# mLSTM attention and two feed-forward stages on one core: the values' product in three 16-bit products, small VectorE work on GpSimd in the source's order, last weight rows loaded once, a fifth row buffer

## The chip, the cores and the metric

The kernel runs on one core of a Trainium2 chip (trn2). The metric is the device time of one execution in microseconds; a kernel's time is the median of its runs. In a profile the engines are PE (TensorE, with PEld for its weight loads), DVE (VectorE), ACT (ScalarE), POOL (GpSimd) and SP (SyncE, which here only issues DMAs). Each engine works through its own queue in order.

## What is computed

Three stages follow each other. First a gated recurrent attention over B, H, S, D = 4, 8, 768, 40; then a feed-forward layer over all 3072 tokens (320 to 2048 to 320 with x·sigmoid(x)); then a mixture of 8 experts (320 to 1024 to 320), in which each token goes to one expert.

```python
for t in range(S):                                  # attention, all b and h
    m_new = np.maximum(f_gate[:, :, t] + m, i_gate[:, :, t])
    f_stab, i_stab = np.exp(f_gate[:, :, t] + m - m_new), np.exp(i_gate[:, :, t] - m_new)
    C = f_stab[:, :, None, None] * C + i_stab[:, :, None, None] * np.einsum('bhd,bhe->bhde', vt, kt)
    n = f_stab[:, :, None] * n + i_stab[:, :, None] * kt
    y[:, :, t] = o * (C @ qt) / np.maximum(np.abs(n @ qt), 1.0)
x = y.transpose(0, 2, 1, 3).reshape(B * S, H * D)
h = x @ w_in;  x = (h / (1 + np.exp(-h))) @ w_out   # first feed-forward layer
expert = argmax(x @ w_gate)                         # the mixture
out = gate * (np.maximum(x @ w1[expert], 0) @ w2[expert])
```

## The kernel before, in words

**Attention** is done in chunks of 128 steps: 6 chunks `c` times 4 batches `b`, so 24 units, each with all 8 heads. A unit has these parts. `prep_qk` splits k and q into 16-bit high and low halves and turns them with a DMA transpose. `load_lam` and `mask_lam` fetch and mask a 128x1024 table of log weights (the mask on POOL, L207), `prep_exp` takes its exponent on ACT (eight instructions, L241). `at_S` multiplies k by q on PE (two groups of four heads), and DVE multiplies the product by the weights in place (L296), which gives the float32 matrix P in the `lam` buffer. `at_I` adds what earlier chunks left (L304, L308). `at_C` updates the state C (24 16-bit products of 41 columns, L353 to L355; before it DVE multiplies the old state by a decay, L359; afterwards L367, L370, L375 and two DMAs). **`at_PV` multiplies P by v in float32** (L318, eight products, two PE passes each), then DVE divides (L324 to L340) and copies 64 columns (L341). `at_X` turns the result for the next stage (L394).

**The first layer** runs over 6 chunks of 512 tokens and 16 blocks `f` of 128 hidden columns. For each block, `l1` does eight 512-column products (L959), ACT the tanh (L975), DVE the product (L978), ACT the 16-bit high half (L983), DVE the low half (L986), and `l2`, two blocks later, twelve products of 328 columns (L1003 to L1005; in part of chunk 0 float32, L1000).

**What sets the order.** The attention of chunk c+1 runs beside the first layer of chunk c. The table `plan` gives each part a position; `f` has two positions, so one chunk has 32. A unit starts (`at_S`) at its position p, eight after the one before it; what a part returns runs one position later (`run_late`). Chunk 0 is ordered by a scheduler; from chunk 1 on PE, ACT, DVE and SP run in the source's order (`by_hand`, L1060), while POOL's order is still the scheduler's. The routing of a finished chunk, `rows`, is put at positions 5, 7, ... 19 of the next chunk, two apart: `experts`, `scale`, `weights`, `place` (two PE products, L877 and L878, into one of the two `ps_at` buffers), then four `halves`, each of which makes a row of 386 words on ACT and DVE (L919 to L928) and scatters it with an indirect DMA from POOL (L929) into `rows_x`.

**The experts** come last: 28 slots of 128 rows. For a slot, `fetch` reads a register, turns 128 rows with a DMA transpose (L1189) and gets two columns (L1194), `m_half` does 32 products of 128 columns (L1209) twice, `m_l2` 24 of 320 columns (L1228 to L1230), and POOL scatters the result (L1240). Rows have four buffers (`xT_b`, L1182): `get(i + 3)` fetches for three slots ahead. Beside this, weights of the experts that don't fit are loaded in 32 pieces by `load_w` (three DMAs: two thirds of w1, **its last 64 rows twice, into both halves of the partitions**, and w2), split on ACT (L552, L553) and DVE (L556 to L564). All these DMAs are on SP's queue:

```python
for i in range(2, len(line)):
    get(i + 3)
    t = half(i, 0); low_and_load(); t()
    if i > 5 and i % 2: split()
    t = half(i, 1); t()
    if i > 5 and i % 2: low_and_load()
    if i == 3: later_slots()
    split()
    if more and i > 4: load(more.pop(0))
    second(i - 1)
```

Of the kernel before, what the change touches and what calls it, by code (L numbers as in the profile page):

```python
# [19 lines left out]
SQ = 256.0  # L20
SX = 2.0**8
# [12 lines left out]
def mlstm_moe_kernel(ctx, tc, q, k, v, ig, fg, og, w_in, w_out, w_gate, w1, w2, out):  # L34
# [106 lines left out]
    q_ld, k_ld, o_ld = [turns([carve(ATTN, (H, D)) for _ in range(3)]) for _ in range(3)]  # L141
# [10 lines left out]
    y_b = turns([carve(FIRST, (384,)), const.tile([128, 384], F32, name="y2")])  # L152
# [133 lines left out]
    def at_S(c, b, g):  # L286
        u = st[c, b]
        if c == 0:
            ps = ps_l1.tile([128, 4, CH], F32, tag="l1", name="ps_s")
        else:  # L290
            ps = ps_at.tile([128, 4, CH], F32, tag="at", name="ps_s")
        for j in range(4):
            h = 4 * g + j
            nc.tensor.matmul(ps[:, j, :], u["kT"][0:120, h, :], u["qT"][0:120, h, :], start=True, stop=True)
        lt = u["lam"][:, 4 * g:4 * g + 4, :]
        return lambda: nc.vector.scalar_tensor_tensor(  # L296
            out=lt, in0=ps, scalar=1.0 / (SQ * SQ), in1=lt, op0=ALU.mult, op1=ALU.mult
        ) and None
# [15 lines left out]
    def at_PV(c, b):  # L314
        u = st[c, b]
        pv = ps_at.tile([128, H, D1], F32, tag="at", name="ps_pv")
        for h in range(H):
            nc.tensor.matmul(pv[:, h, :], u["lam"][:, h, :], u["v"][:, h, :], start=True, stop=True)  # L318

        def tail():  # L320
# [12 lines left out]
            nc.vector.tensor_scalar(out=den, in0=den, scalar1=1.0, scalar2=2.0, op0=ALU.max, op1=ALU.mult)  # L333
# [7 lines left out]
            nc.vector.tensor_copy(out=yt[:, DM:384], in_=yt[:, 256:DM])  # L341
# [3 lines left out]
    def at_C(c, b):  # L345
# [11 lines left out]
        if c > 0:  # L357
            o = c * BH + b * H
            nc.vector.tensor_tensor(  # L359
# [172 lines left out]
    def load_w(k, g, e, ts=None):  # L532
# [6 lines left out]
        if isinstance(e, int):  # L539
            nc.sync.dma_start(out=t[:, 0:2, :], in_=w1[e, 0:256, cs].rearrange("(j p) f -> p j f", p=128))  # L540
            nc.sync.dma_start(out=t[:, 2, :], in_=bcast0(w1[e, 256:320, cs], 2))
            nc.sync.dma_start(out=t2, in_=w2[e, cs, :].rearrange("(j p) d -> p j d", p=128))
        else:
            ee = bass.ds(e, 1)
            nc.sync.dma_start(out=t[:, 0:2, :], in_=w1[ee, 0:256, cs].rearrange("e (j p) f -> p (e j) f", p=128))
            nc.sync.dma_start(out=t[:, 2, :], in_=w1[ee, 256:320, cs].to_broadcast([2, 64, GF]))
# [4 lines left out]
        def go():  # L551
            nc.scalar.activation(out=o1[:, 0:3, :], in_=t, func=AF.Copy, scale=SW1)  # L552
            nc.scalar.activation(out=o2[:, :, 0, :], in_=t2, func=AF.Copy, scale=SW2)  # L553

            def tail():
# [5 lines left out]
                    out=o1[64:128, 2, :], in0=t[64:128, 2, :], scalar=SW1, in1=o1[64:128, 2, :],  # L561
# [9 lines left out]
    with contextlib.nullcontext():  # L571

        wg_t = const.tile([128, 3, E], F32, name="wg_t")
        with tc.tile_pool(name="gate", bufs=1) as gp:
# [105 lines left out]
            def first(b, g):  # L680
                return first_d(b, g, sel, parts, idb, mneg)

            run = lambda ts: [t() for t in ts]
# [24 lines left out]
            v0 = prep_v(0, 0)  # L708
            p0 = at_PV(0, 0)
# [8 lines left out]
            v1 = prep_v(0, 1)  # L718
            p1_ = at_PV(0, 1)
# [20 lines left out]
            v2 = prep_v(0, 2)  # L740
            p2 = at_PV(0, 2)
# [13 lines left out]
            v3 = prep_v(0, 3)  # L755
            p3 = at_PV(0, 3)
# [19 lines left out]
                out=E_t[:, 1:, :], in0=E_t[:, 1:, :], scalar1=1.0 / (SQ * SQ), scalar2=None, op0=ALU.mult  # L776
# [20 lines left out]
        for n in range(B, NC * B):  # L797
# [8 lines left out]
            at(p - 5, mask_lam, *cb)  # L806
            at(p - 3, prep_exp, *cb, 0)
            at(p - 2, prep_exp, *cb, 1)
            at(p, at_S, *cb, 0)
            at(p + 1, at_S, *cb, 1)  # L810
# [33 lines left out]
        def rows(c, b0=0, b1=B):  # L844
# [70 lines left out]
            def halves(b):  # L915
# [5 lines left out]
                def tail():  # L921
# [21 lines left out]
        at(2 * NF * (NC - 1) + 23, lambda: fetch_early())  # L943
# [238 lines left out]
        xT_b = turns([x[:, 0:6, :] for x in Ks[1:] + Qs + Ks[:1]])  # L1182
# [115 lines left out]
        with tc.manual_schedule(engines=by_hand):  # L1298
# [29 lines left out]
            get(NE + 1)  # L1328
            for i in range(2, len(line)):
                get(i + 3)  # L1330
# [57 lines left out]
```

## Time and profile before

| | us |
|---|---|
| median of 3 runs (lowest to highest) | 732.72 (732.57 to 733.4) |
| the profiled execution, its own time | 736.41 |
| its span on the core | 734.7 |
| PE busy in the span | 671.2 (91%) |
| DVE busy | 529.7 (72%) |
| ACT busy | 372.7 (51%) |
| POOL busy | 100.6 (14%) |
| PE, first layer's L959 | 193.1 |
| PE, values' product L318 | 51.2 (modelled, 384 pieces) |
| PE, experts' L1209 | 110.0 (1792 pieces) |

Busy time is the union of an engine's instructions. PE's instructions overlap in their pipeline, so a piece that reads 0.3 us can follow the one before it 0.14 us later: what a product costs is read from the distance between starts, not from its length. The span is cut into stages by the instructions that run in it: attention alone up to about 47 us, first layer with attention up to about 435, first layer alone up to about 509, experts up to 723, and then the last scatter.

### The profile page before, as it was taken

To read this page: it belongs to the slowest core of one execution; us is meant where nothing else is said; L and a number is where in the kernel's file an instruction comes from. 1 tells how busy PE (TensorE), PEld (TensorE's weight loads), DVE (VectorE), ACT (ScalarE), POOL (GpSimd) and SP (SyncE) were. 2 spreads that over 40 slices of the span, in tenths; PEclk is the share of its full clock that TensorE was granted. 3 is DMA by queue.
4 is the path that set the end of the run, shared out by engine and by line. 5 is a ranking of instruction groups with operands and counts; after the bars stand their busy time and mean duration, and the time that the engine had idled before them with its cause. 6 is when DMAs were issued, how large, how long until landed. Compare 5 with 4: busy or idle time off the path is not lost.

```text
span 734.7 us, 15579 instructions
## 1 busy us (share of the span) xinstructions
PE 671.2 (91%) x5840; PEld 480.0 (65%) x5840; DVE 529.7 (72%) x1262; ACT 372.7 (51%) x816; POOL 100.6 (14%) x134
## 2 busy tenths in 40 slices
PE   3868899999899989998999999999999898998993
PEld 2734666776476655665666665556888786877882
DVE  7775779987888787799887975975677655665631
ACT  4644365655575655675676635564334333533410
POOL 3100011100121002110210110020311111111111
PEclk9758599999999988999999999999999999999998
DMA  8768979884565655976587520544279799999900
GB/s 158 128 150 205 201 144 212 196 198 88 106 139 127 138 100 106 166 149 131 116 180 162 133 80 14 128 146 105 80 145 194 166 189 171 186 170 190 160 24 15
DMA packets 242828, 102.82 MB, mean 140 GB/s; under 512 B 181141, under 2 KB 236632, under 8 KB 242744
## 3 DMA queue, kind: packets, MB, share of 16 engines
q1 hardware_dynamic: 239380, 92.98, 63.8%
q0 software_dynamic: 2880, 8.68, 3.5%
q8 instruction: 48, 0.79, 0.5%
q14 instruction: 36, 0.29, 0.2%
q10 hardware_dynamic: 484, 0.08, 0.1%
HBM read 71.64 MB, written 11.59 MB: 113 GB/s over the span
## 4 chain that ended last, share of the span: by engine, by line
PE 70%; DVE 13%; DMA 8%; ACT 3%; SPq 3%; issue 2%; POOL 0%; POOLq 0%; DVEq 0%; ACTq 0%
PE ps_h L959 19%; PE ps_m L1209 12%; PE ps_y L1003 5%; PE ps_y L1005 5%; PE ps_y L1004 5%; PE ps_pv L318 5%; DMA Ks<-rows_x 3%; PE ps_y L1000 3%; PE ps_m L1228 3%; PE ps_m L1230 3%; PE ps_m L1229 3%; DMA Qs<-rows_x 2%; PE ps_wg L517 1%; DMA wi<-in_moe_w_in_dram 1%; DMA w_all<-lam_d 1%
## 5 line engine op out<-in xcount | busy, mean ns | idle before, releaser
L959 PE MATMUL ps_h<-w_all 128*128 128x512 f16 x768 | 193.1, 392 | 8.2 <-ACT w_all L466 5.1
L959 PEld LDWEIGHTS <-w_all 128*128 128x128 f16 x768 | 73.5, 100 | 85.1 <-issue 10.6
L1209 PEld LDWEIGHTS <-w_all 128*128 128x128 f16 x1792 | 106.8, 101 | 19.1 <-DMA Ks<-rows_x 9.9
L1005 PE MATMUL ps_y<-w_all 128*128 128x328 f16 x332 | 101.1, 305 | 0.3 <-DVE w_all L986 0.3
L1004 PE MATMUL ps_y<-w_all 128*128 128x328 f16 x332 | 101.1, 305 | 0.0
L1003 PE MATMUL ps_y<-w_all 128*128 128x328 f16 x332 | 100.9, 305 | 0.0
L1214 ACT ACTIVATE hh<-ps_m 128x512 f16<-128x512 f32 x56 | 33.3, 596 | 126.5 <-PE ps_m L1209 114.9
L975 ACT ACTIVATE w_all<-ps_h 128x512 f32<-128x512 f32 x83 | 49.2, 592 | 67.0 <-PE ps_h L959 66.8
L978 DVE SCALAR_TENSOR_TENSOR w_all<-w_all,ps_h 128x512 f32<-128x512 f32 x83 | 56.7, 683 | 29.3 <-ACT w_all L975 28.0
L1215 DVE SCALAR_TENSOR_TENSOR hl<-ps_m,hh 128x512 f16<-128x512 f32 x56 | 38.6, 690 | 48.5 <-ACT hh L1214 48.1
L983 ACT ACTIVATE w_all<-w_all 128x512 f16<-128x512 f32 x83 | 51.6, 622 | 30.7 <-DVE w_all L978 28.9
L1229 PE MATMUL ps_m<-w_all,hh 128*128 128x320 f16 x224 | 67.0, 299 | 0.0
L1230 PE MATMUL ps_m<-w_all,hl 128*128 128x320 f16 x224 | 67.0, 299 | 0.0
L1228 PE MATMUL ps_m<-w_all,hh 128*128 128x320 f16 x224 | 67.0, 299 | 0.0
L1209 PE MATMUL ps_m<-Ks,w_all 128*128 128x128 f16 x896 | 55.9, 226 | 8.9 <-DMA Ks<-rows_x 6.9
L986 DVE SCALAR_TENSOR_TENSOR w_all<-w_all 128x512 f16<-128x512 f32 x83 | 57.9, 697 | 5.6 <-ACT w_all L983 5.3
L1209 PE MATMUL ps_m<-Qs,w_all 128*128 128x128 f16 x896 | 54.1, 222 | 6.0 <-DMA Qs<-rows_x 4.2
L1240 POOL DMA_INDIRECT out_dram<-ym,sid x28 | 32.0, 1142 | 169.5 <-DVE sid L1239 153.7
L318 PEld LDWEIGHTS ps_pv<-w_all 128*128 128x128 f32 x384 | 51.2, 210 | 4.3 <-issue 1.7
L318 PE MATMUL ps_pv<-w_all 128*128 128x41 f32 x384 | 51.2, 296 | 0.4 <-DVE w_all L296 0.4
L241 ACT ACTIVATE w_all<-w_all,bias_t 128x128 f32<-128x128 f32 x160 | 50.2, 391 | 2.4 <-POOL w_all L207 2.3
L207 POOL TENSOR_SCALAR_AFFINE_SELECT w_all<-w_all 128x1024 f32<-128x1024 f32 x20 | 22.8, 1142 | 183.1 <-DMA w_all<-lam_d 130.0
(219 smaller groups left out, 1159.6 us busy)
## 6 DMA issues: line engine op xcount, KB each, us to landing
e<-in_moe_w_dram SPq DMA_DIRECT2D x35, 320.0 KB
w_all<-lam_d SPq DMA_DIRECT2D x20, 512.0 KB
e<-in_moe_w_dram SPq DMA_DIRECT2D x35, 256.0 KB
w_all<-in_moe_w_out_dram SPq DMA_DIRECT2D x16, 320.0 KB
e<-in_moe_w_dram SPq DMA_DIRECT2D x35, 128.0 KB
w_all<-in_moe_w_dram SPq DMA_DIRECT2D x13, 320.0 KB
wi<-in_moe_w_in_dram SPq DMA_DIRECT2D x8, 512.0 KB
w_all<-in_k_dram SPq DMA_DIRECT2D x24, 160.0 KB
```

Source lines behind the costliest of these rows:

```text
L318: nc.tensor.matmul(pv[:, h, :], u["lam"][:, h, :], u["v"][:, h, :], start=True, stop=True)
L959: nc.tensor.matmul(ps, a, x, start=(i == 0), stop=(i == len(terms) - 1))
L978: nc.vector.scalar_tensor_tensor(out=th, in0=th, scalar=1.0, in1=ps, op0=ALU.add, op1=ALU.mult)
L983: nc.scalar.activation(out=gh, in_=th, func=AF.Copy, scale=SG)
L986: nc.vector.scalar_tensor_tensor(out=gl, in0=th, scalar=SG, in1=gh, op0=ALU.mult, op1=ALU.subtract)
L1003: nc.tensor.matmul(ps, gh[:, ts], woh[:, f, :], start=(f == 0), stop=False)
L1004: nc.tensor.matmul(ps, gh[:, ts], wol[:, f, :], start=False, stop=False)
L1005: nc.tensor.matmul(ps, gl[:, ts], woh[:, f, :], start=False, stop=(f == NF - 1))
L1209: nc.tensor.matmul(ps[:, jj, :], w1c[k][:, a, f * 128:f * 128 + 128], x[:, m, :], start=(n == 0), stop=(n == len(terms) - 1),)
L1228: nc.tensor.matmul(ps, hh[:, f, :], w[:, 0, :], start=(f == 0), stop=False)
L1229: nc.tensor.matmul(ps, hh[:, f, :], w[:, 1, :], start=False, stop=False)
L1230: nc.tensor.matmul(ps, hl[:, f, :], w[:, 0, :], start=False, stop=(f == NF2 - 1))
```

## The change

1. **Values' product.** P is scaled by 64 and split on its way: ACT copies it to 16 bit (`ph_b`, one buffer for all units), POOL subtracts that from P and leaves the 16-bit rest in the `lam` buffer. v is split likewise by `split_v`, at position p (ACT high half, DVE low half). `at_PV` then has three 16-bit products for each head in place of one float32 product. The scale is taken out with the denominator.
2. **POOL** takes the decay of C (L359), the copy of 64 columns of y (L341) and the three copies of a row (L926 to L928). From chunk 1 on its order is the source's as well. The mask moves from position p-5 to p-4; `rows` come at 5, 7, 9, 13, 14, 16, 18, 20.
3. **Weights.** The last 64 rows of a piece of w1 are loaded once; ACT converts them with an instruction of their own, and DVE reads them in the lower half and writes the upper.
4. **Rows.** `y2` becomes a row buffer, so there are five, and `get(i + 4)` fetches for four slots ahead. q and k have two load buffers in place of three.

```diff
-    q_ld, k_ld, o_ld = [turns([carve(ATTN, (H, D)) for _ in range(3)]) for _ in range(3)]
+    q_ld, k_ld, o_ld = [turns([carve(ATTN, (H, D)) for _ in range(n)]) for n in (2, 2, 3)]
...
+        pl = u["lam"].rearrange("p h t -> p (h t)").bitcast(F16)[:, 1024 * g:1024 * g + 512]
+        def tail():
+            nc.vector.scalar_tensor_tensor(
+                out=lt, in0=ps, scalar=SP / (SQ * SQ), in1=lt, op0=ALU.mult, op1=ALU.mult
+            )
+            return cast
+        def cast():
+            nc.scalar.copy(out=ph_b[:, hs, :], in_=lt)
+            nc.gpsimd.tensor_tensor(out=u["pl", g], in0=lt, in1=ph_b[:, hs, :], op=ALU.subtract)
+        return tail
+    def split_v(c, b):
+        v = st[c, b]["v"]
+        nc.scalar.activation(out=v1_b, in_=v, func=AF.Copy, scale=SQ)
+        return lambda: nc.vector.scalar_tensor_tensor(
+            out=v2_b, in0=v, scalar=SQ, in1=v1_b, op0=ALU.mult, op1=ALU.subtract
         ) and None
...
-            nc.tensor.matmul(pv[:, h, :], u["lam"][:, h, :], u["v"][:, h, :], start=True, stop=True)
+            nc.tensor.matmul(pv[:, h, :], ph_b[:, h, :], v1_b[:, h, :], start=True, stop=False)
+            nc.tensor.matmul(pv[:, h, :], ph_b[:, h, :], v2_b[:, h, :], start=False, stop=False)
+            nc.tensor.matmul(pv[:, h, :], u["pl", h // 4][:, h % 4, :], v1_b[:, h, :], start=False, stop=True)
...
-            nc.vector.tensor_copy(out=yt[:, DM:384], in_=yt[:, 256:DM])
+            nc.gpsimd.tensor_copy(out=yt[:, DM:384], in_=yt[:, 256:DM])
...
-            nc.vector.tensor_tensor(
+            nc.gpsimd.tensor_tensor(
                 out=C, in0=C, in1=dec[0:D, o:o + H].unsqueeze(2).to_broadcast([D, H, D1]), op=ALU.mult
             )
...
-            nc.sync.dma_start(out=t[:, 2, :], in_=bcast0(w1[e, 256:320, cs], 2))
+            nc.sync.dma_start(out=t[0:64, 2, :], in_=w1[e, 256:320, cs])
...
-            nc.scalar.activation(out=o1[:, 0:3, :], in_=t, func=AF.Copy, scale=SW1)
+            nc.scalar.activation(out=o1[:, 0:2, :], in_=t[:, 0:2, :], func=AF.Copy, scale=SW1)
+            nc.scalar.activation(out=o1[0:64, 2, :], in_=t[0:64, 2, :], func=AF.Copy, scale=SW1)
...
-            at(p - 5, mask_lam, *cb)
+            at(p - 4, mask_lam, *cb)
...
+            at(p, split_v, *cb)
...
-                    nc.vector.tensor_copy(out=row[:, 384:385], in_=r["ls"][:, b:b + 1])
-                    nc.vector.tensor_copy(out=row[:, 385:386], in_=tok[:, c * B + b0 + b:c * B + b0 + b + 1])
-                    nc.vector.tensor_copy(out=r16[:, DM:384], in_=r16[:, 256:DM])
+                    nc.gpsimd.tensor_copy(out=row[:, 384:385], in_=r["ls"][:, b:b + 1])
+                    nc.gpsimd.tensor_copy(out=row[:, 385:386], in_=tok[:, c * B + b0 + b:c * B + b0 + b + 1])
+                    nc.gpsimd.tensor_copy(out=r16[:, DM:384], in_=r16[:, 256:DM])
...
-            for i, fn in enumerate(rows(c)):
-                at(2 * NF * (c + 1) + 5 + 2 * i, fn)
+            for i, fn in zip((5, 7, 9, 13, 14, 16, 18, 20), rows(c)):
+                at(2 * NF * (c + 1) + i, fn)
...
+        all_by_hand = by_hand | {ENG.Pool}
...
-                in_order.enter_context(tc.manual_schedule(engines=by_hand))
+                in_order.enter_context(tc.manual_schedule(engines=all_by_hand))
...
-        xT_b = turns([x[:, 0:6, :] for x in Ks[1:] + Qs + Ks[:1]])
+        xT_b = turns(
+            [Ks[1][:, 0:6, :], y2.bitcast(F16).rearrange("p (j t) -> p j t", j=6)]
+            + [x[:, 0:6, :] for x in Qs + Ks[:1]]
+        )
...
+            get(NE + 2)
             for i in range(2, len(line)):
-                get(i + 3)
+                get(i + 4)
```

How the instructions stand, at the three places that matter most. First POOL's queue beside the row scatters of a chunk. Here `L252` and `L256` weight v for the state, `L207` is the mask, `L929` and `L963` are the scatters. Before:

```order
L252 TENSOR_TENSOR w_all<-w_all,wend_t 128x328
L929 DMA rows_x<-w_all,di 25600x386
L207 AFFINE_SELECT w_all<-w_all 128x1024
L929 DMA rows_x<-w_all,di 25600x386 x2
L252 TENSOR_TENSOR w_all<-w_all,wend_t 128x328
```

Now, where `L313` is the subtraction that gives P's rest, `L384` the decay and `L960` to `L962` the copies of a row:

```order
L256 TENSOR_TENSOR w_all<-w_all,wend_t 128x328
L313 TENSOR_TENSOR w_all<-w_all 128x512
L960 COPY w_all<-ls 128x1
L961 COPY w_all<-tok 128x1
L962 COPY w_all<-w_all 128x64
L963 DMA rows_x<-w_all,di 25600x386
L313 TENSOR_TENSOR w_all<-w_all 128x512
L384 TENSOR_TENSOR w_all<-w_all,dec 40x328
```

The second half of P's rest now stands behind a row scatter on POOL.

Second, ACT's queue in one unit. `L983` and `L1017` are the high half of the first layer, `L975` and `L1009` its tanh, `L218` to `L247` (now `L222` to `L251`) are `prep_qk` and the tanh of the output gate. Before:

```order
L975 ACTIVATE w_all<-ps_h 128x512
L218 ACTIVATE Ks_110<-w_all 128x8x2x40
L221 ACTIVATE Qs_108<-w_all 128x8x80
L247 ACTIVATE w_all<-w_all 128x320
L983 ACTIVATE w_all<-w_all 128x512
L975 ACTIVATE w_all<-ps_h 128x512
```

Now, where `L318` is the high half of v and `L312` the 16-bit copy of P:

```order
L318 ACTIVATE w_all<-w_all 128x328
L1017 ACTIVATE w_all<-w_all 128x512
L1009 ACTIVATE w_all<-ps_h 128x512
L222 ACTIVATE Ks_109<-w_all 128x8x2x40
L225 ACTIVATE Qs_107<-w_all 128x8x80
L251 ACTIVATE w_all<-w_all 128x320
L312 CAST w_all<-w_all 128x512
L1017 ACTIVATE w_all<-w_all 128x512
L312 CAST w_all<-w_all 128x512
L1009 ACTIVATE w_all<-ps_h 128x512
```

Each unit has three instructions more there, and the two copies of P stand ahead of a high half and of a tanh.

Third, SP's queue at the start of the experts: the fetches of rows (`Ks_109` is slot 6 before and slot 7 now, `Ks_110` slot 7 before) and the first weights after them. Before:

```order
L1189 DMA_TRANSPOSE Ks_109<-rows_x 128x6x128
L1194 ISA
L1194 DMA xms<-rows_x 128x2
L540 DMA e_6240<-in_moe_w_dram 128x2x256
L541 DMA e_6240<-in_moe_w_dram 128x1x256
L542 DMA e_6240<-in_moe_w_dram 128x2x320
L1186 TENSOR_LOAD kofi
L1186 ISA x2
L1189 ISA
L1189 DMA_TRANSPOSE Ks_110<-rows_x 128x6x128
```

Now:

```order
L1227 DMA_TRANSPOSE Qs_108<-rows_x 128x6x128
L1232 ISA
L1232 DMA xms<-rows_x 128x2
L1224 TENSOR_LOAD kofi
L1224 ISA x2
L1227 ISA
L1227 DMA_TRANSPOSE Ks_109<-rows_x 128x6x128
L1232 ISA
L1232 DMA xms<-rows_x 128x2
L565 DMA e_6796<-in_moe_w_dram 128x2x256
L566 DMA e_6796<-in_moe_w_dram 64x256
L567 DMA e_6796<-in_moe_w_dram 128x2x320
```

From here on every fetch stands where the fetch of the slot before it stood, with one more fetch ahead of the weights.

## Rows read from the trace of the kernel before

**Rows 1.** The page, part 1: busy time, share and instructions of each engine.
```profile
PE 671.2 (91%) x5840; PEld 480.0 (65%) x5840; DVE 529.7 (72%) x1262; ACT 372.7 (51%) x816; POOL 100.6 (14%) x134
```
**Rows 2.** The page, part 4: the chain that ended last, by engine.
```profile
PE 70%; DVE 13%; DMA 8%; ACT 3%; SPq 3%; issue 2%; POOL 0%; POOLq 0%; DVEq 0%; ACTq 0%
```
**Rows 3.** Windows of one unit each: length, busy times, PE clock, DMA share, GB/s.
```profile
257.90:282.80 24.90, 22.58 (x143) 13.92 (x142) 18.45 (x49) 11.87 (x27) 3.39 (x4) 0.79 0.50 109
282.80:299.90 17.10, 17.10 (x141) 11.23 (x139) 15.83 (x40) 12.00 (x27) 4.09 (x4) 1.00 0.70 124
299.90:317.00 17.10, 17.10 (x141) 11.23 (x139) 13.22 (x27) 11.16 (x24) 2.07 (x2) 1.00 0.90 176
...
334.10:354.40 20.30, 17.41 (x143) 11.19 (x141) 18.37 (x51) 11.73 (x26) 1.57 (x2) 1.00 0.51 108
```
**Rows 4.** The chain in order of time: start, length, instruction and count.
```profile
271.98 3.27 PE ps_pv L318 x16
...
293.30 1.71 PE ps_pv L318 x16
```
**Rows 5.** Timeline of PE: start, length, engine, line, operation, operands, shapes, count.
```profile
322.89 0.20 PE L353 MATMUL ps_c<-w_all,Ks 128*40 128x41 f16 x1
...
323.59 0.10 PEld L1003 LDWEIGHTS <-w_all 128*128 128x128 f16 x1
...
425.26 0.36 PE L304 MATMUL ps_it<-w_all 120*128 120x41 f16 x8
...
425.47 1.89 PE L959 MATMUL ps_h<-w_all 128*128 128x512 f16 x8
```
**Rows 6.** Waits from 180 to 434 us: in total, times, longest.
```profile
PE ps_r L877 <- DVE w_all L367: 2.9, 2, 1.5
PE ps_r L877 <- DVE w_all L296: 2.7, 1, 2.7
```
**Rows 7.** Timeline of DVE and POOL.
```profile
277.28 0.49 DVE L340 TENSOR_TENSOR w_all<-w_all,den 128x320 f32<-128x320 f32 x1
...
296.95 0.95 POOL L252 TENSOR_TENSOR w_all<-w_all,wend_t 128x328 f32<-128x328 f32 x1 [5.85 <-DMA w_all<-in_v_dram]
...
297.34 0.91 DVE L340 TENSOR_TENSOR y<-y,den 128x320 f32<-128x320 f32 x1
```
**Rows 8.** Groups by line: shapes, count, busy us, mean ns, idle before and releasers.
```profile
L252 POOL TENSOR_TENSOR w_all<-w_all,wend_t 128x328 f32<-128x328 f32 x20 | 15.6, 782 | 136.5 <-DMA w_all<-in_v_dram 98.6 <-DVE w_all L978 9.5 <-DVE w_all L296 9.2
...
L983 ACT ACTIVATE w_all<-w_all 128x512 f16<-128x512 f32 x83 | 51.6, 622 | 30.7 <-DVE w_all L978 28.9
...
L359 DVE TENSOR_TENSOR w_all<-w_all,dec 40x328 f32<-40x328 f32 x12 | 6.0, 501 | 0.0
```
**Rows 9.** Timeline of one unit: P's second half is finished; its product begins.
```profile
425.75 0.68 DVE L296 SCALAR_TENSOR_TENSOR w_all<-ps_s,w_all 128x512 f32<-128x512 f32 x1
...
430.92 1.87 PE L318 MATMUL ps_pv<-w_all 128*128 128x41 f32 x16
```
**Rows 10.** The chain in order of time, experts.
```profile
550.90 3.57 PE ps_m L1209 x64
...
557.74 3.57 PE ps_m L1209 x64
...
678.36 7.17 DMA Ks<-rows_x
...
692.59 3.57 PE ps_m L1209 x64
```
**Rows 11.** Timeline of SP's queue: issues of fetches and weights.
```profile
525.57 1.28 SPq L1189 DMA_TRANSPOSE Ks<-rows_x  x1
...
528.30 1.24 SPq L1189 DMA_TRANSPOSE Qs<-rows_x  x1
...
571.75 0.40 SPq L540 DMA_DIRECT2D e<-in_moe_w_dram  x1
...
575.68 0.68 SPq L540 DMA_DIRECT2D w_all<-in_moe_w_dram  x1
```

More of the change, by code (lines that the diff above doesn't have):

```diff
@@ L20 @@
 SQ = 256.0
+SP = 2.0**6
 SX = 2.0**8
@@ L140, in mlstm_moe_kernel @@
     Va = [carve(ATTN, (H, D1)) for i in range(NV)]
-    q_ld, k_ld, o_ld = [turns([carve(ATTN, (H, D)) for _ in range(3)]) for _ in range(3)]
+    q_ld, k_ld, o_ld = [turns([carve(ATTN, (H, D)) for _ in range(n)]) for n in (2, 2, 3)]
+    ph_b = carve(ATTN, (H, CH), F16)
+    v1_b, v2_b = [carve(ATTN, (H, D1), F16) for _ in range(2)]
     lam_b = turns([carve(ATTN, (H, CH)) for _ in range(2)])
@@ L151, in mlstm_moe_kernel @@
     vw_b, hb_b = carve(FIRST, (H, D1)), carve(FIRST, (H, D1))
-    y_b = turns([carve(FIRST, (384,)), const.tile([128, 384], F32, name="y2")])
+    y2 = const.tile([128, 384], F32, name="y2")
+    y_b = turns([carve(FIRST, (384,)), y2])
     cl_b = carve(FIRST, (H, D1), F16)[0:D]
@@ L294, in at_S @@
             nc.tensor.matmul(ps[:, j, :], u["kT"][0:120, h, :], u["qT"][0:120, h, :], start=True, stop=True)
-        lt = u["lam"][:, 4 * g:4 * g + 4, :]
+        hs = slice(4 * g, 4 * g + 4)
+        lt = u["lam"][:, hs, :]
+        pl = u["lam"].rearrange("p h t -> p (h t)").bitcast(F16)[:, 1024 * g:1024 * g + 512]
+        u["pl", g] = pl.rearrange("p (h t) -> p h t", t=CH)
+        def tail():
[10 more added lines that the diff above has]
+        nc.scalar.activation(out=v1_b, in_=v, func=AF.Copy, scale=SQ)
         return lambda: nc.vector.scalar_tensor_tensor(
-            out=lt, in0=ps, scalar=1.0 / (SQ * SQ), in1=lt, op0=ALU.mult, op1=ALU.mult
+            out=v2_b, in0=v, scalar=SQ, in1=v1_b, op0=ALU.mult, op1=ALU.subtract
         ) and None
@@ L332, in tail @@
             )
-            nc.vector.tensor_scalar(out=den, in0=den, scalar1=1.0, scalar2=2.0, op0=ALU.max, op1=ALU.mult)
+            nc.vector.tensor_scalar(out=den, in0=den, scalar1=SP * SQ, scalar2=2.0, op0=ALU.max, op1=ALU.mult)
             nc.vector.reciprocal(out=den, in_=den)
@@ L560, in tail @@
                 nc.vector.scalar_tensor_tensor(
-                    out=o1[64:128, 2, :], in0=t[64:128, 2, :], scalar=SW1, in1=o1[64:128, 2, :],
+                    out=o1[64:128, 2, :], in0=t[0:64, 2, :], scalar=SW1, in1=o1[0:64, 2, :],
                     op0=ALU.mult, op1=ALU.subtract,
@@ L681, in first, with run @@
                 return first_d(b, g, sel, parts, idb, mneg)
-            run = lambda ts: [t() for t in ts]
+            def run(ts):
+                while ts:
+                    ts = [t for t in [x() for x in ts] if callable(t)]
             k0 = prep_qk(0, 0)
@@ L708, in mlstm_moe_kernel @@
             v0 = prep_v(0, 0)
+            now(split_v, 0, 0)
             p0 = at_PV(0, 0)
@@ L718, in mlstm_moe_kernel @@
             v1 = prep_v(0, 1)
+            now(split_v, 0, 1)
             p1_ = at_PV(0, 1)
@@ L740, in mlstm_moe_kernel @@
             v2 = prep_v(0, 2)
+            now(split_v, 0, 2)
             p2 = at_PV(0, 2)
@@ L755, in mlstm_moe_kernel @@
             v3 = prep_v(0, 3)
+            now(split_v, 0, 3)
             p3 = at_PV(0, 3)
@@ L775, in mlstm_moe_kernel @@
             nc.vector.tensor_scalar(
-                out=E_t[:, 1:, :], in0=E_t[:, 1:, :], scalar1=1.0 / (SQ * SQ), scalar2=None, op0=ALU.mult
+                out=E_t[:, 1:, :], in0=E_t[:, 1:, :], scalar1=SP / SQ, scalar2=None, op0=ALU.mult
             )
```

4 lines of the change are left out of this document (2 added, 2 removed).

## The prediction

> **What bounds the kernel now.** I read the busy times first, then the chain that ended last, then windows of one unit each, then the timelines of the places that the change touches. The busy times say that PE works in 671.2 of 734.7 us, far more than any other engine [rows 1], and the chain says where the rest is: 70% of it is PE, 13% DVE, 8% DMA [rows 2]. So there are two questions: what does PE have to do less of, and where does the chain leave PE?
>
> The windows answer for the middle of the kernel. A period of eight positions with one attention unit takes 17.10 us, and PE is busy in all of it at a granted clock of 1.00, the higher level of 2.4 GHz [rows 3]. There every microsecond taken from PE is a microsecond of time, as long as DVE, with 13.22 to 15.83 us in the same periods, can follow. Where one chunk goes over into the next it is different: 24.90 and 20.30 us for the same work, in the first at a mean clock of 0.79 [rows 3]. The list of waits names part of it: `place` on PE (L877) waits for a PSUM buffer that DVE still has to empty, 2.9 us in two waits and 2.7 us in one [rows 6].
>
> In the experts a slot without a stall takes 6.84 us, from 550.90 to 557.74. From 550.90 to 692.59 there are 18 slots, which would be 123.1 us and are 141.7: 18.6 us are lost, and the chain shows on what, the row transposes on SP's queue (the one at 678.36 takes 7.17 us to land) [rows 10].
>
> **The values' product.** At full clock it takes PE 1.71 us, at half clock 3.27 us [rows 4]. The new one has 24 16-bit pieces of 41 columns. The state's product has just that count and width: 0.70 us from 322.89 to 323.59. `at_I`, with weights of 128 columns as here, takes 0.21 us for eight, which would be 0.63 for 24 [rows 5]. I take 0.70, so a unit gains 1.01 us, or 3.27 − 1.40 = 1.87 at half clock. Twenty units lie beside the first layer; with two of them at half clock that is 18 × 1.01 + 2 × 1.87 = 21.9 us.
>
> Not all of it comes through, because of **DVE's port**. POOL gets two subtractions of 128x512 a unit. A 128x328 `tensor_tensor` takes it 782 ns [rows 8]; by the elements 1.22 us each. With the decay (another 328 columns, 0.78) and the copies POOL has some 3.4 us more a unit. Now, a DVE division with both operands in SBUF takes 0.49 us alone and 0.91 when POOL's L252 is running: L252 starts at 296.95, lasts 0.95, and both end within 0.4 us of each other [rows 7]. So POOL's work can hold up DVE's. DVE's own count is about even: the low half of v costs about 0.49, as an operation of its kind [rows 7], the decay gives back 0.50 [rows 8]. If less than half of POOL's 3.4 us catches a DVE operation, 1.5 us of waiting are added. A unit with 13.22 us of DVE work bears this, one with 15.83 comes to 17.3, above the shorter period of 16.1 us. Each of the five chunk changes has about one such unit, so I take off 5 × 1.01 = 5: **+16.9** stays (ends: 0, if DVE decides everywhere, and 21.9).
>
> **The new chain before the product.** P's second half is finished at 425.75 + 0.68 = 426.43, and its product begins at 430.92, so there are 4.5 us [rows 9]. Needed are one cast on ACT (0.62, as L983 of the same shape) and one subtraction on POOL (1.22): 1.84 us [rows 8]. In a free unit this is covered. Behind the waiting product on PE stand `l2` of the block and the next `l1`, and behind those ACT's tanh and DVE's product; behind POOL's subtraction stand the decay, for which the state's update on DVE waits, and the next mask, for which the exponent waits. In a row-put unit the second subtraction stands behind a scatter. If all of POOL's 4.09 us [rows 3] stood ahead, 4.09 + 1.84 − 4.5 = 1.4 us would be late, in five units 7; the order shows one row ahead, not all. **−2** (ends −7 and 0). ACT gets two casts and the high half of v, some 1.7 us on 12.00 of 17.10 [rows 3, 8]: room.
>
> **`place` later.** At position 13 it comes behind the product, when the buffers are read. The 5.6 us of rows 6 are the upper end, zero the lower (the buffer may again be taken). I take **+2**, since in the window around 270 us other waits remain.
>
> **The experts.** SP's queue is behind, so an earlier place in it is a gain once. The fetch issued at 678.36 is that of slot 23; after the change slot 24's stands there, one slot earlier than before. One more fetch ahead costs 528.30 − 525.57 = 2.73 us of issue; a load takes 3.9 us of the queue (571.75 to 575.68) [rows 11], and by bytes one eleventh of it goes (64 of 704 KB), 0.36 us. With 21 loads up to there that is 7.6 us at most; I count 5, as issues also wait for buffers. So 678.36 + 2.73 − 5 + 7.17 = 683.3 is when slot 24's rows land. Without a stall it would start at 550.90 + 123.1 = 674.0, so it is 9.3 us late in place of 18.6: **+9.3** [rows 10, 11]. Without any relief from the bytes it is 4.3, with no stall left 18.6.
>
> **The start and the rest.** In the first chunk's units the latency of 1.84 us is added and the product gives 1.87 at its low clock: 0, with two units either way (±3.7) as ends. ACT's extra instruction for the weights, the halves on DVE, the mask one position later and the two load buffers for q and k are counted at nothing: ACT has 5 us to spare in a period [rows 3], and a mask or a load that came late would show as exponents waiting, an end I leave to the rivals.
>
> **Sum:** 16.9 − 2 + 2 + 9.3 + 0 = 26.2. The profiled execution took 736.4 by its own time, so 710.2; it stands 3.7 above the median of the runs, and so **706.5 us**.
>
> **Rivals.**
> *All comes through* (0.12): DVE keeps up, `place` never waits, the rows are always there. 736.4 − 21.9 − 5.6 − 18.6 = 690.3, 686.6 by the median. For it speaks that DVE has idle time in all four windows; against it that rows still land 7.17 us after issue.
>
> *DVE becomes the bound* (0.20): every microsecond of new POOL work holds DVE for one. In the four windows DVE has 65.9 us in 79.4; with 4 × 3.4 it is at 79.5 [rows 3]. Then a shorter product gives PE nothing, and only the experts gain: 736.4 − 9.3 = 727.1, 723.4 by the median. Rows 7 speak for it, that a good part of DVE's work reads PSUM speaks against it. The Trainium skill, "SBUF — State Buffer", section "SBUF: two separate sides", has a rule that would bring this about: a DVE operation with two SBUF inputs and a GpSimd operation exclude each other for a whole instruction, the second blocked until the first is done. The trace agrees as far as it goes: 0.91 against 0.49.
>
> *The product waits for POOL* (0.09), the slower one: at the chunk changes ACT and POOL are behind, the second subtraction misses the product by more than the 4.5 us of cover, PE idles and its clock falls. A chunk change in which that happens costs what the window at 257.90 cost, 24.90 − 17.10 = 7.8 us [rows 3]. Five more of those are 39 us, against the 26.2: 749.2, 745.5 by the median. It decides from four such hits on. Against it speak the 4.5 us of slack.
>
> *Weight loads set the pace* (0.03): if each of the 24 pieces waited for its load of 128 columns (0.10 us [rows 5]), the product would take 2.4 in place of 1.71 us; 20 × 0.69 = 14 lost, 9.3 gained in the experts: 741, 737 by the median. Rows 5 speak against it, with eight in 0.21. The Trainium skill, "TensorE: Matmul & The Clock Gate", section "LDWEIGHTS (loading the stationary operand)", gives about 107 ns for 128 columns; by it the product would be an estimated 2.56 us and the loss 17 us.
>
> *The fetch's place is worth nothing* (0.06): the transposes land as late, measured from their slot, because the bytes' way and not the queue is the limit. 736.4 − 16.9 = 719.5, 715.8 by the median.
>
> **How the numbers follow.** The forecast gets 0.50. Its own ends reach from some 698 (+18.6 in the experts) to 714 (half of the product's gain lost). From 688, just above the first rival, to 726, behind DVE's, nearly everything but the two slower cases (0.12) and part of the first rival is inside. About 0.2% is what a measurement of this kernel can tell from no change. Slower by more: 0.09 + 0.03, less a little for the milder half of them, 0.11; the same 0.02; faster 0.87.
>
> **What would show it.** Right: windows of 16.1 us with PE full; the values' product at about 0.7; DVE operations with two SBUF operands that end with POOL's L313; P's rest done before the product; slots of 6.84 us for longer, and the last stalls shorter by half. Wrong: PE waiting for POOL's subtraction at each unit, a state update that waits for the decay, windows still of 17 us with DVE full, or row transposes that take longer than 7.17 us because one more is in flight.

## The result, and the profile after

The changed kernel takes 710.05 us (median of 4 runs, 705.36 to 712.16) against 732.64 us before beside it; the ratio is 0.9683 with the interval 0.9632 to 0.9734. The forecast was 706.5, in the range 688 to 726. The total came out as forecast, by luck: its parts did not, and most of what follows is about that. (Medians here are over all runs; the ratios leave disturbed runs out, so the two need not agree to the last per mille.)

The page, part 1, of the changed kernel:

```profile
PE 635.4 (89%) x6032; PEld 443.3 (62%) x6032; DVE 548.2 (77%) x1174; ACT 408.0 (57%) x936; POOL 209.1 (29%) x294
```

Beside [rows 1], PE has 35.8 us less, DVE 18.5 more, and POOL twice its work. Part 4, the chain by engine:

```profile
PE 56%; DVE 21%; issue 6%; DMA 5%; POOL 4%; ACT 3%; SPq 2%; POOLq 0%; DVEq 0%; ACTq 0%
```

PE was 70% of the chain [rows 2], now it is 56%; DVE went from 13 to 21%, POOL from nothing to 4%, and DMA fell from 8 to 5%. So somewhere PE stopped being what everything waits for. Where, the stages tell (starts read from both traces, us):

| | before | after | difference |
|---|---|---|---|
| first `l1` | 47.2 | 55.0 | +7.8 |
| ninth block of chunk 0 | 110.3 | 105.3 | -5.0 |
| first block of chunk 1 | 161.3 | 162.7 | +1.4 |
| last block of chunk 5 | 502.6 | 497.1 | -5.5 |
| first product of the experts | 509.4 | 503.8 | -5.6 |
| last `m_half` product | 716.4 | 691.7 | -24.7 |

By these two profiles all that lies before the experts gave 5.6 us, where the forecast had 16.9 (16.9 - 2 + 2 + 0), and the experts gave 19.1, where it had 9.3. Two errors of about ten microseconds cancel. How much of the 5.6 is the change's is open: by the medians of runs 1 and 2 below it is 1.7 us, not told from nothing.

**The experts** run without a stall. The chain in order of time:

```profile
572.16 3.57 PE ps_m L1247 x64
...
579.00 3.57 PE ps_m L1247 x64
...
688.33 3.57 PE ps_m L1247 x64
```

From 579.00 to 688.33 are 16 slots of 6.83 us, and no transpose stands in the chain between them, as the one at 678.36 did [rows 10].

**Beside the first layer** PE works less and waits more. The stretch from the first block of chunk 1 to the first product of the experts, which is the same part of the program each time: before, in run 1 below (whose attention is that of before), and after (length; busy time of PE, PEld, DVE, ACT, POOL; clock, DMA share, GB/s):

```profile
161.35:509.38 348.03, 338.42 (x2495) 215.29 (x2493) 278.75 (x683) 205.15 (x443) 43.85 (x46) 0.98 0.56 124
```

```profile
153.35:496.21 342.86, 333.15 (x2495) 212.80 (x2493) 279.15 (x683) 206.78 (x459) 44.11 (x46) 1.00 0.54 122
```

```profile
162.70:503.81 341.11, 317.58 (x2573) 192.12 (x2572) 286.55 (x606) 224.58 (x500) 117.61 (x167) 0.98 0.55 121
```

PE's work fell by 20.8 us against the first and by 15.6 against the second; its idle time rose by 14, from 9.6 and 9.7 to 23.5. The saving was made, and most of it lost in place: the stretch is 6.9 or 1.7 us shorter. The list of waits of PE, 160 to 434 us, after:

```profile
PE ps_pv L341 <- DVE w_all L392: 7.4, 6, 2.0
PE ps_x L419 <- DVE w_all L331: 7.4, 3, 4.8
PE ps_it L327 <- DVE w_all L306: 3.7, 4, 1.7
PE ps_c L378 <- DVE w_all L306: 2.4, 2, 2.2
```

The waits of `place` [rows 6] are gone; these have come, but for the third row, which stood there before with 2.9 us. The first row is the new product, and what it waits for is not P's rest but L392, the update of the state, which has to empty one of the two `ps_at` buffers. The timeline shows what L392 waits for. POOL, and then DVE, at such a place (start, length):

```profile
211.12 2.28 POOL L313 TENSOR_TENSOR w_all<-w_all 128x512 f16<-128x512 f32 x2
...
213.93 0.23 POOL L962 COPY w_all<-w_all 128x64 f16<-128x64 f16 x1
214.61 1.00 POOL L963 DMA_INDIRECT rows_x<-w_all,di  x1 [0.45 <-POOL w_all L962]
215.64 0.75 POOL L384 TENSOR_TENSOR w_all<-w_all,dec 40x328 f32<-40x328 f32 x1
```

```profile
211.86 1.97 DVE L956 SCALAR_TENSOR_TENSOR w_all<-w_all,sc 128x320 f16<-128x320 f32 x1
216.42 0.49 DVE L392 SCALAR_TENSOR_TENSOR w_all<-ps_c,w_all 40x328 f32<-40x328 f32 x1 [2.60 <-POOL w_all L384]
216.84 1.14 DVE L1020 SCALAR_TENSOR_TENSOR w_all<-w_all 128x512 f16<-128x512 f32 x1
```

Two things are to be seen. The decay, L384, stands on POOL behind both subtractions, a row's copies and its scatter; DVE stands still for 2.60 us, with the first layer's L1020 behind it in its queue. And L956, usually 0.54 us long, takes 1.97 beside the subtractions and the copy behind them.

### The profile page after: what moved, and what is told of

Same layout as the page of the kernel before. It is cut to its first block, busy times and chain, and to the rows that moved or that the text cites. A ratio compares the mean times of both kernels' runs of the same rounds, so it can differ in the third digit from the quotient of the medians.

```text
span 710.5 us, 16146 instructions
## 1 busy us (share of the span) xinstructions
PE 635.4 (89%) x6032; PEld 443.3 (62%) x6032; DVE 548.2 (77%) x1174; ACT 408.0 (57%) x936; POOL 209.1 (29%) x294
## 3 DMA queue, kind: packets, MB, share of 16 engines
q1 hardware_dynamic: 236980, 89.84, 59.4%
## 4 chain that ended last, share of the span: by engine, by line
PE 56%; DVE 21%; issue 6%; DMA 5%; POOL 4%; ACT 3%; SPq 2%; POOLq 0%; DVEq 0%; ACTq 0%
PE ps_m L1247 13%; PE ps_h L993 13%; PE ps_m L1266 4%; PE ps_m L1268 4%; PE ps_m L1267 4%; PE ps_y L1037 3%; PE ps_y L1039 3%; PE ps_y L1038 3%; PE ps_y L1034 2%; DVE w_all L1020 2%; DMA w_all<-in_moe_w_out_dram 2%; DVE w_all L1012 2%; PE ps_wg L542 1%; DVE w_all L306 1%; POOL w_all L313 1%
## 5 line engine op out<-in xcount | busy, mean ns | idle before, releaser
L993 PEld LDWEIGHTS <-w_all 128*128 128x128 f16 x768 | 72.9, 99 | 78.8 <-issue 8.8
L1247 PEld LDWEIGHTS <-w_all 128*128 128x128 f16 x1792 | 102.4, 98 | 4.4 <-issue 1.3
L313 POOL TENSOR_TENSOR w_all<-w_all 128x512 f16<-128x512 f32 x48 | 62.1, 1301 | 122.1 <-ACT w_all L312 121.5
L1020 DVE SCALAR_TENSOR_TENSOR w_all<-w_all 128x512 f16<-128x512 f32 x83 | 62.9, 758 | 8.2 <-ACT w_all L1017 8.0
L1012 DVE SCALAR_TENSOR_TENSOR w_all<-w_all,ps_h 128x512 f32<-128x512 f32 x83 | 56.5, 681 | 15.6 <-ACT w_all L1009 15.4
L1017 ACT ACTIVATE w_all<-w_all 128x512 f16<-128x512 f32 x83 | 51.7, 623 | 28.4 <-DVE w_all L1012 27.0
L1009 ACT ACTIVATE w_all<-ps_h 128x512 f32<-128x512 f32 x83 | 48.9, 589 | 29.1 <-PE ps_h L993 28.6
L1247 PE MATMUL ps_m<-Qs,w_all 128*128 128x128 f16 x768 | 45.0, 219 | 1.9 <-DVE hl L1253 1.9
L1037 PEld LDWEIGHTS <-w_all 128*128 128x128 f16 x332 | 32.4, 98 | 17.0 <-ACT w_all L1017 1.5
L1038 PEld LDWEIGHTS <-w_all 128*128 128x128 f16 x332 | 32.6, 98 | 15.2
L1039 PEld LDWEIGHTS <-w_all 128*128 128x128 f16 x332 | 32.6, 98 | 14.9 <-DVE w_all L1020 1.0
```

Source lines behind the costliest of these rows:

```text
L313: nc.gpsimd.tensor_tensor(out=u["pl", g], in0=lt, in1=ph_b[:, hs, :], op=ALU.subtract)
L993: nc.tensor.matmul(ps, a, x, start=(i == 0), stop=(i == len(terms) - 1))
L1012: nc.vector.scalar_tensor_tensor(out=th, in0=th, scalar=1.0, in1=ps, op0=ALU.add, op1=ALU.mult)
L1017: nc.scalar.activation(out=gh, in_=th, func=AF.Copy, scale=SG)
L1020: nc.vector.scalar_tensor_tensor(out=gl, in0=th, scalar=SG, in1=gh, op0=ALU.mult, op1=ALU.subtract)
L1037: nc.tensor.matmul(ps, gh[:, ts], woh[:, f, :], start=(f == 0), stop=False)
```

## The experiments

Which of the two is what PE's saving was lost to? **Theory Q**: the order of POOL's queue, above all the decay behind subtractions and scatters. **Theory L**: what the prediction calls DVE's port, that is, DVE's operations take longer beside POOL's. And for the experts: the fetch one slot earlier (**F**), or the smaller loads (**W**). The runs came in three groups of four, each group beside its own runs of the kernel before (medians 729.3, 729.4, 728.0); times are compared within a group.

### Taking the change apart

**1. The experts' parts alone**, on the kernel before: the weights' last rows once, the fifth row buffer.

```diff
-            nc.sync.dma_start(out=t[:, 2, :], in_=bcast0(w1[e, 256:320, cs], 2))
+            nc.sync.dma_start(out=t[0:64, 2, :], in_=w1[e, 256:320, cs])
...
+            get(NE + 2)
             for i in range(2, len(line)):
-                get(i + 3)
+                get(i + 4)
```

> The kernel before with the weights' last rows once and the fifth row buffer, nothing of the attention. By the two traces the experts took 207.1 us before (first L1209 at 509.4 to last at 716.4) and 187.9 after, 19.2 less; all before that only 5.6 less. Theory: the parts add up, so 732.6 - 19.2 = 713.4, no stalled slot from 558 on. Rival: the experts' gain leans on the attention's part (DMA that is done earlier): then less than 12 us, over 720. By the prediction's own step (+9.3): 723.3.

Measured: 713.4 (702.7 to 715.5), ratio 0.9811 (0.9759 to 0.9862); the experts took 194.5 us from the first to the end of the last product, 213.8 before and 194.6 with the whole change. The gain of the experts needs nothing of the attention's part.

**2. Four row buffers**, the changed kernel otherwise:

```diff
...
-            get(NE + 2)
             for i in range(2, len(line)):
-                get(i + 4)
+                get(i + 3)
```

> The changed kernel with four row buffers and the fetch three slots ahead, the weights' last rows still loaded once. Theory F: it is the fetch one slot earlier that ended the stalls; without it slots wait again and 8 to 19 us come back, 718 to 729. Rival W: the smaller loads on SP's queue ended them; then 710 to 712. By the prediction's step 5 us came from the bytes and 4.3 from the place, that is 714.

Measured: 711.7, ratio 0.9755 (0.9699 to 0.9812); experts 194.9 us. Theory F falls: where the loads are small, the earlier fetch changes the experts by 0.3 us, less than two profiles of the changed kernel differ by (194.6 and 196.1). In the same group run 1 had 713.4, so the whole attention part moved the median by 1.7 us, which the two intervals do not tell from nothing.

**3. The last rows twice**, with five buffers, beside the changed kernel once more (**4**):

```diff
-            nc.sync.dma_start(out=t[0:64, 2, :], in_=w1[e, 256:320, cs])
+            nc.sync.dma_start(out=t[:, 2, :], in_=bcast0(w1[e, 256:320, cs], 2))
...
```

> The changed kernel with the weights' last 64 rows loaded twice again, and with the five row buffers. The run with four buffers had no stall (194.9 us of experts). Theory W (the smaller loads alone ended the stalls): the experts are back at about 210 to 214 us, less what a fetch one slot earlier brings once (by the prediction 4.3): 720 to 729. Rival E (either of the two is enough): 194 to 197 us of experts, 710.

> The changed kernel as it is, on the chip of the next three runs, to stand beside them: 705 to 712, the experts 194.6 us from the first to the last product. Both theories expect the same.

Measured: 728.5, ratio 1.0018 (0.9965 to 1.0072), experts 212.8 us; the changed kernel beside it 711.3, ratio 0.9708 (0.9630 to 0.9785). Theory W holds, and more than that: without this one edit the rest of the change is worth nothing that these runs can tell. The earlier fetch alone leaves the experts at 212.8 us against 213.8 before. Its chain again shows transposes between the products:

```profile
581.42 7.19 DMA Ks<-rows_x
588.66 3.75 PE ps_m L1246 x64
...
596.58 7.79 DMA y<-rows_x
604.42 3.75 PE ps_m L1246 x64
...
612.43 9.98 DMA Qs<-rows_x
```

**5. 128 different rows.** One eleventh of the bytes is little for 18 us, so this run tells bytes from the way in which they are read. It does so for the first 28 of the 48 pieces: the next four, of the last expert, read 64 rows twice as in run 3, and the last 16, whose expert is read from a register, stay loaded once, as in the change.

```diff
-            nc.sync.dma_start(out=t[0:64, 2, :], in_=w1[e, 256:320, cs])
+            if e < E - 1:
+                r0 = e * DM + 256
+                nc.sync.dma_start(out=t[:, 2, :], in_=w1.rearrange("e r f -> (e r) f")[r0:r0 + 128, cs])
+            else:
+                nc.sync.dma_start(out=t[:, 2, :], in_=bcast0(w1[e, 256:320, cs], 2))
```

> The changed kernel, but the load of a piece's last 64 rows takes 128 rows again: in place of the same 64 a second time, the 64 that follow them in memory (the next expert's first rows, which nothing reads; for the last expert the same 64 twice). Bytes, packets and partitions are those of the run with rows loaded twice (experts 212.8 us). Theory B (the bytes and packets fill the DMA engines): 210 to 214 us of experts again, 725 to 729 in all, the 256-byte packets of the row transposes at 80 ns or more. Theory R (reading the same rows twice is what is slow): 194 to 198 us, 711, those packets at 38 to 45 ns.

Measured: 713.0, ratio 0.9821 (0.9780 to 0.9861), experts 194.7 us, no stall. Other than expected, the run as a whole does not carry as many bytes as run 3, so the comparison is made where it does. From the issue of the 20th piece to that of the 29th, nine pieces with equal bytes, packets and partitions, SP's queue took 50.4 us in run 3 (534.3 to 584.7) and 32.6 here (535.0 to 567.6); the changed kernel took 31.3. The four pieces after them, read twice here too, took 21.5 us here and 17.1 in the changed kernel. So it is the way and not the bytes: theory R. For the last 16 pieces the two were not told apart. The windows of 536 to 566 us, of run 3, of run 5 and of the changed kernel:

```profile
536.00:566.00 30.00, 29.61 (x372) 25.27 (x371) 19.75 (x37) 11.06 (x18) 5.87 (x5) 1.00 0.99 171
```

```profile
536.00:566.00 30.00, 29.61 (x371) 25.23 (x369) 19.73 (x36) 12.88 (x26) 5.86 (x5) 1.00 0.99 247
```

```profile
536.00:566.00 30.00, 29.62 (x378) 25.43 (x377) 19.68 (x38) 12.17 (x24) 5.42 (x5) 1.00 0.99 247
```

The DMA engines read as full in all three (0.99), but move 171 GB/s in the first and 247 in the others. PE comes to stand still only later. The windows of 580 to 620 us, of before, of run 3 and of the changed kernel:

```profile
580.00:620.00 40.00, 34.37 (x409) 29.04 (x406) 23.48 (x44) 15.25 (x24) 6.62 (x6) 0.96 1.01 171
```

```profile
580.00:620.00 40.00, 34.67 (x440) 29.34 (x439) 22.96 (x43) 16.33 (x25) 4.87 (x5) 1.00 1.04 169
```

```profile
580.00:620.00 40.00, 40.00 (x514) 34.53 (x511) 26.84 (x49) 19.86 (x39) 6.97 (x6) 1.00 0.90 206
```

What differs is to be seen in the packet records of one load in a quiet stretch (the second load of each trace, near 265 us): the 1 KB packets in progress at a time, every half microsecond from the first packet on.

```
                     packets  0.25 0.75 1.25 1.75 2.25 2.75 3.25 3.75 4.25   all in us
before                  384     10   15    6    2    2    2    2    1    2        4.39
run 3, rows twice       384      8   17    5    2    2    2    2    1    2        4.29
run 5, 128 rows         384      4   18   17    3    0    0    0    0    0        2.08
after, rows once        320     13   13    6    0    0    0    0    0    0        1.72
```

The load that reads 64 rows twice has a first axis of length 2, and its packets run two at a time for some three microseconds, where those of other loads run 13 to 18 at a time at their peak. One packet takes no longer: the median is 46 ns in all four, so it is not the second reading of a row that is slow. With a load and a half per slot, what else is on the queue comes late: the 256-byte packets, those of the row transposes, took 87 ns on the mean in run 3 from 536 to 566 us, 42 in run 5 and 37 in the changed kernel, with the same median of 18. In run 5 itself the mean rose to 77 from 568 to 589 us, beside the four pieces that are read twice (40 in the changed kernel). That these packets wait behind the two is the likely link; the records do not say which engine a packet was on. The Trainium skill, "DMA: Bandwidth & Descriptors", section "Rules for kernel authors", states just this: a leading broadcast of c copies confines the whole transfer to at most c of the 16 engines. The trace agrees, with its 2 packets at a time.

### Where the product's gain went

A run's time also holds chunk 0 and the landing of the last scatter, 2.5 to 4.6 us from its start in these profiles, whatever the edit. So beside the medians the stretch from the first block of chunk 1 to the experts' first product is given, from one profile each:

| | us |
|---|---|
| attention as before: before, run 1 | 348.0, 342.9 |
| attention as changed: five profiles (the change, runs 2 to 5) | 341.1 to 341.6 |
| run 6 | 344.8 |
| run 7 | 338.6 |
| run 8 | 337.8 |
| run 9 | 337.1 |
| run 10 | 340.6 |

**6. The product twice over**, from the second chunk on:

```diff
-        for h in range(H):
+        for h in [*range(H)] * (2 if c else 1):
             nc.tensor.matmul(pv[:, h, :], ph_b[:, h, :], v1_b[:, h, :], start=True, stop=False)
```

> The changed kernel with the new values' product done twice over from the second chunk on (48 pieces, the second pass starts afresh), about 0.6 us more of PE in each of 20 units, DVE, ACT and POOL as they are. If PE still sets the period beside the first layer, 12 us more, 722 to 724. If DVE's and POOL's chains set it (the forecast's second rival, which gives a shorter product no worth), 0 to 4 us more, 711 to 715.

Measured: 715.4, ratio 0.9840 (0.9789 to 0.9890), against 713.0 of run 5 in its group, whose attention is the change's. Twelve microseconds of PE's work more cost 2.4; in the stretch 16 of the 20 units, with 9.8 us more, cost 3.5. PE does not set the period there for the most part. A shorter product is then unlikely to have paid in full, but a longer one does not show that it would have paid nothing.

**7. The decay early** on POOL, ahead of the subtractions:

```diff
...
+            if cb[0] < NC - 1:
+                at(p, decay_C, *cb)
```

> The changed kernel with the decay of C on POOL put at position p, ahead of P's subtractions and of the row scatters behind which it stands now. PE lost 7.4 us from 160 to 434 waiting in L341 for the buffer that L392 empties, and L392 waited for the decay. Theory Q (order on POOL's queue): these waits go, 710 - 7 = 703. Theory L (DVE waits for the port that it shares with POOL): POOL's work is as long, DVE's operations are as late, 709 to 711.

Measured: 706.3, ratio 0.9674 (0.9618 to 0.9729); run 2 in its group had 711.7, and the runs of the two do not overlap. The wait that was PE's first row:

```profile
PE ps_pv L341 <- DVE w_all L394: 2.5, 3, 1.5
```

It fell from 7.4 to 2.5 us, and DVE's wait of 7.9 us for the decay is gone. DVE's operations were no shorter: what they took over their usual length (the lower quartile of their line) is 24.6 us from 180 to 434 in the changed kernel and 32.0 here. So this gain came from the order of the queue: theory Q. Its size is less than the 5.4 us between the medians: the stretch is 2.9 us shorter than in run 2, as other waits of PE grew, and of the 4.8 us between the two profiles 2.1 lie behind the last `m_half` product, which the edit does not touch.

**8. The subtractions on DVE**, one position later:

```diff
-            nc.gpsimd.tensor_tensor(out=u["pl", g], in0=lt, in1=ph_b[:, hs, :], op=ALU.subtract)
+            return low
+        def low():
+            nc.vector.scalar_tensor_tensor(
+                out=u["pl", g], in0=lt, scalar=1.0, in1=ph_b[:, hs, :], op0=ALU.mult, op1=ALU.subtract
+            )
```

> The changed kernel with both subtractions of P's rest on DVE, one position later, in place of POOL (62.1 us in 48). DVE gets 48 x 0.68 = 33 us of work more, 27 of it beside the first layer. Theory L: the operations that waited for POOL's subtraction (24.6 us over their usual length from 180 to 434, 8.9 before the change) are back at their usual length and POOL's queue is short, so DVE has 16 us less of waiting for 20 more of work: 706 to 712. Theory Q: the decay is no more behind the subtractions: 705. Rival: DVE's own work decides: 548 + 33 us busy, 715 or more.

Measured: 704.7 (703.2 to 705.1), ratio 0.9667 (0.9616 to 0.9718). It is the fastest median of all runs, 7.0 below run 2 beside it; the stretch is 3.7 us shorter. The lengthening of DVE's operations fell to 15.2 us (8.9 before the change), DVE's wait for the decay from 7.9 to 2.0. Both theories can have a share: PE's second row of waits, L419, fell from 7.4 to 3.1 us here, but only to 5.8 in run 7. At its longest wait in the changed kernel, 4.77 us up to 266.93, DVE had been busy almost without a pause since 261.42, and three of its operations there took 2.9 us over their usual length beside POOL's.

**9. Both edits together** (7 and 8).

> The changed kernel with the decay early on POOL and the subtractions on DVE. Alone they gave 706.3 and 704.7 where four row buffers, the change otherwise, gave 711.7. Theory Q (in both the decay came free of the queue): no more than the better one, 704 to 705. Theory L (the second one took the port away from POOL's long work, a second gain): they add up, about 700.

Measured: 705.8, ratio 0.9647 (0.9576 to 0.9719), 5.5 below the changed kernel beside it. The medians do not add up, as theory Q has it: in both the decay came free. The stretch is 4.4 us shorter than in run 2, where the two alone gave 2.9 and 3.7. What PE still waits for is DVE; its waits in this run:

```profile
PE ps_it L332 <- DVE w_all L306: 4.9, 5, 2.1
PE ps_c L390 <- DVE w_all L306: 4.6, 5, 1.7
PE ps_y L1048 <- DVE w_all L1029: 3.2, 4, 1.3
```

**10. All of it on DVE**: subtractions, decay and copies.

```diff
...
-            nc.gpsimd.tensor_tensor(
+            nc.vector.tensor_tensor(
                 out=C, in0=C, in1=dec[0:D, o:o + H].unsqueeze(2).to_broadcast([D, H, D1]), op=ALU.mult
...
```

> The changed kernel with the subtractions, the decay, the copies of y and of the rows all on DVE; POOL has only the masks, the weighting of v and the scatters, as before the change. With the subtractions alone on DVE it was 704.7. Theory Q (what POOL still had there costs nothing): DVE's 0.5 + 0.2 us a unit more and the rows' copies, some 20 us of DVE in all, come in part on top: 708 to 715. Theory L (each small piece on POOL holds DVE about as long as it would take there): 703 to 706.

Measured: 711.4, ratio 0.9801 (0.9759 to 0.9844), 1.6 below run 5 beside it. Here DVE is busy for 236.2 of 254 us from 180 to 434, 230.6 in run 8. Its interval of ratios lies above that of run 8, so with the subtractions on DVE the decay and copies are better on POOL; that DVE's own work is the next bound fits this, but was not tried further. The 708 to 715 of theory Q hold.

### The start

**11. The first chunk's product in float32**, its copies on POOL, and **12. the same with these copies on DVE**, and the subtractions of the later chunks on DVE:

```diff
-            return cast
+            return cast if c else None
...
+            if c == 0:
+                nc.tensor.matmul(pv[:, h, :], u["lam"][:, h, :], u["v"][:, h, :], start=True, stop=True)
+                continue
```

> The changed kernel with the values' product of the first chunk in float32 as before the change, without split and subtraction there; later chunks as changed. The first l1 began at 47.2 before and 55.0 after; the prediction counted the start at nothing. Theory S (the start is late because of the split, and it stays): block 0 at 47 and 4 to 8 us off the total, 702 to 706. Rival D (what comes next waits for other things, the first layer's weights, or for the clock): block 0 at 47, but block 16 and the total unchanged, 709 to 711.

> The subtractions on DVE from the second chunk on, and the first chunk's product in float32 without a split and with its copies of y on DVE, as before the change. The first l1 began at 59.4 us where the subtractions were on DVE throughout, and at 47.2 before the change. If the start's delay stays in the total: 698 to 702. If what follows waits for the first layer's weights or the clock anyway, as the run with float32 and the copies on POOL suggests: 704 to 708.

Measured: run 11 713.9, ratio 0.9782 (0.9688 to 0.9875), not better than the 711.3 beside it; its first `l1` is at 52.6 and not at 47. Run 12 708.2 (704.8 to 713.4), ratio 0.9774 (0.9703 to 0.9845), 4.7 below run 5 beside it, with ranges that overlap, and no better than run 8. Its first `l1` is at 45.2 where run 8 had 59.4, and yet chunk 1 begins at 158.2 against 158.5. Fourteen microseconds at the start are gone within one chunk: rival D holds, as far as one profile each and these medians tell. What the first chunk waits for instead was not settled.

## Why the prediction was right in its total and wrong in its parts

**The values' product itself: right.** The 24 pieces start from 323.32 to 323.90, so they take 0.61 us with the last step; 0.70 was taken. The stretch from chunk 1 to the experts has 16 units, 16.2 us by the 1.01 each that was worked out; PE's work there fell by 15.6 to 20.8.

**What comes through of it: wrong.** The step that failed is the +16.9 after five microseconds for DVE's port, together with the -2 for the chain ahead of the product: 1.7 us by runs 1 and 2, 5.6 by the two profiles. The second rival, that DVE and POOL come to bound this stage, was priced at no gain from the product and is nearer; run 6 bears it out for the most part. But its mechanism was only half right. DVE's operations are lengthened: L956 took 1.97 us, and with L313 off POOL the sum of it fell from 24.6 to 15.2 us (run 8). Yet run 7 gained without shortening them, by an order that the forecast had before its eyes: it named the decay behind the subtractions and the state's update that waits for it, and counted the decay as 0.50 us less for DVE and 0.78 more for POOL, with no wait. Both edits together give back 4.4 us of the stretch; the rest of what was lost PE still waits out on DVE (run 9), and how it divides was not settled. The wait that was priced, for P's rest, is not there from 160 to 434 us (2.9 us in three waits before 60 us); the product waits for the PSUM buffer of the step before it.

**`place`: right in itself, worth nothing.** Its 5.6 us of waits are gone, the upper end. The time is lost to other waits at the same chunk changes, such as the 4.8 us of L419.

**The experts: wrong twice.** The 4.3 us for an earlier place in SP's queue measured 0.3 with the small load (run 2) and 1.0 with the old one (run 3). The 5 us for the bytes were not theirs: nine pieces with as many bytes kept within 1.3 us of the changed kernel's pace (run 5). The backlog on the queue was read rightly, its cause was not: a load whose packets run two at a time. The forecast counted that load by its bytes, 64 of 704 KB, where its packets, two at a time in the trace of before already, were what to count. The first rival's 18.6 us for the experts is what came.

**The start: its sum fits, its course does not.** The first layer began 7.8 us late, beyond the end given; runs 11 and 12 speak for it, by one profile each, that this does not reach chunk 1.

## What to carry to other kernels

A transfer's cost is not its bytes: look at how many of its packets run at a time, and give a DMA a long first axis; loads with a broadcast as the first axis, of length 2, held up the row transposes on the same queue. Before an instruction is moved to an idle engine, list what stands ahead of it there and who waits for its result, however short it is; the decay, 0.50 us on DVE and 0.75 on POOL, held DVE for 2.60 us at the place shown. And where work is taken from the engine that bounds, double it once as a test: if little of that comes through, the bound has moved.

## What the runs showed of the hardware that was not expected

The DMA share of a window reads 0.99 whether 171 or 247 GB/s are moved (536 to 566 us, runs 3 and 5); a full share did not mean that the engines could do no more.

DVE operations of a few elements are held up beside POOL too. Two of 128x4, usually 0.17 us, in the changed kernel, with POOL's rows first. L942 ends with the two subtractions (264.14 and 264.11 us), L944 with the mask L211 (265.86 and 265.85), so it was not the subtractions alone:

```profile
261.01 3.10 POOL L313 TENSOR_TENSOR w_all<-w_all 128x512 f16<-128x512 f32 x2 [7.50 <-ACT w_all L312]
264.07 0.73 POOL L384 TENSOR_TENSOR w_all<-w_all,dec 40x328 f32<-40x328 f32 x1
264.76 1.09 POOL L211 TENSOR_SCALAR_AFFINE_SELECT w_all<-w_all 128x1024 f32<-128x1024 f32 x1
```

```profile
263.23 0.91 DVE L942 TENSOR_SCALAR ls<-ls 128x4 f32<-128x4 f32 x1
...
264.38 1.48 DVE L944 TENSOR_TENSOR ls<-ls,si 128x4 f32<-128x4 f32 x1
```

The start spreads by itself. In run 1, whose instructions up to there are those of before, the ninth block began at 101.0 us and not at 110.3; from 80 to 100 us the granted clock was 1.00 there and 0.68 in the profile of before. Nine microseconds lie between two executions of the same instructions, more than the 5.6 that the two profiles give to all that lies before the experts.
